# Linear attention and a leaky-ReLU MLP on one core: a new order table, other engines and ring places for its steps, and the last-but-one quarter of the result stored in two parts

## The chip, the cores and the metric

The kernel runs on one core of one Trainium2 chip. The metric is device time in microseconds of one execution. The kernel before took 276.14 us (median of three runs, 275.97 to 276.53). Comparisons below are made against that median; the trace comes from one profiled execution of its own.

## The reference

Two stages run one after the other. The first is linear ("cosformer") attention over 8 batches, 8 heads, 576 positions and 64 features:

```
r = relu(x);  phi(x) = [r*cos(theta_s), r*sin(theta_s)]        # 128 features, for q and k
kv  = einsum('bhsf,bhsd->bhfd', phi(k), v);  z = sum_s phi(k)
out = einsum('bhsf,bhfd->bhsd', phi(q), kv) / (phi(q).z + 1e-6)
```

The second takes the result as 4608 tokens of 512 features through an MLP of width 2048:

```
h = x @ w_in;  g = max(0.01*h, h);  result = g @ w_out
```

Inputs and result are float32 in DRAM; the kernel multiplies in float16 and accumulates in float32.

## The kernel before

**Tiling.** The 4608 tokens are cut into nine groups. Groups 0 to 7 are the first 512 positions of one batch each; group 8 collects the last 64 positions of all eight batches. Each group passes through the same stages, and several groups are in flight at once. Group 0 uses plain matmuls (its first MLP layer is `ffn1`, its second `ffn2`). Groups 1 to 8 use a scheme with seven block products instead of eight for each MLP layer (`ffn1s`, `ffn2s`), with sums of blocks made ahead of them and behind them on the vector engines.

**What sets the order.** The kernel is written as some 1430 named steps, and the string `ORDER` lists the names. The loop at the end of the kernel issues each step in that order, so `ORDER` fixes the order of instructions on every engine's own queue. A name can carry an engine (`:D` VectorE, `:A` ScalarE, `:P` GpSimd) and a place (`@n`) in a ring of buffers; a step that takes a place waits until the former user of that place is done. Each engine works strictly down its list: an instruction that waits holds up all behind it. SyncE (SP) issues nearly all DMAs, in the order of the table too.

**Names of the steps used below.** The first number is the group.

- `i.n`: one matmul of zeros (128x512, `ps_idle`, L298), which keeps TensorE busy while data are awaited. `idle(14)` issues fourteen of them before the table begins.
- `Lq`, `Lk`, `Lv`, `Lw1`, `Lw2`: first loads of q, k, v and the two weights; `lq`, `lk`, `lv`: those of later groups (`lq8.0` to `lq8.3`: group 8's rows of q, two DMAs each). `cw`, `w`: casts of the weights to float16; `w3.2` is the cast of the last piece of `w_out`, which `Lw2.3.2` loads.
- `rq`, `rk`, `q`, `kt`, `v`: relu, angles and casts of q, k and v. `kv`, `ko`: the sum over positions and its copy out.
- `qT`: DMA transpose of q's features. `n`, `N`: the attention's product on TensorE and its division on VectorE (`den`, `rden`, `xs`). `xT`: DMA transpose of a group's attention output into the layout that the MLP reads (group 1 does it on TensorE: `xt`, and `xo` copies it out).
- `X`: sums of blocks of xT. `fg.u.1` to `fg.u.7`: the seven products of the first layer for quarter u of the width; `b`, `s`, `u` copy accumulators, `y`, `z` add them, `a`, `c`, `e`, `d` apply the leaky ReLU and write g.
- `S`: sums of blocks of g. `T1` to `T4`: sums of blocks of w_out, made once. `Fg.n.tt.h`: half h of product n for half tt of the tokens in the second layer, four matmuls each. `M`: a sum kept for later; `O`: a quarter of the result copied or added into SBUF; `D`: its store.

**Group 8's end.** Its four result quarters are `O8.2`, `O8.5`, `O8.4`, `O8.3`. `O8.5` and `O8.3` are made and stored in two halves (`result_apart`, `store_apart`), since their accumulators lie apart; `O8.2` and `O8.4` are made whole (`result`, `store`). A store of group 8 is two DMAs, one issued by SP and one by ScalarE.

Of the kernel before, what the change touches and what calls it, by code (L numbers as in the profile page):

```python
# [31 lines left out]
Lk0.0@2 rk0.0:A Lq0.0@1 Lq0.1 Lv0.0@3 kt0.0.0 rq0.0:A qt0.1.0@1 i.6@1 kt0.0.1 rq0.1:D v0.0:D Lv0.1  # L32
Lk0.1 v0.1:P qo0.1.0:A rk0.1:A i.2@1 qt0.0.0@1 qo0.0.0:D i.8@0 i.10@0 i.4@0 i.11@0 qt0.0.1 i.14@0
qo0.0.1:A Lk0.3 rk0.3:P i.7@0 qt0.1.1@0 i.5@1 i.9@1 kt0.1.1 kt0.1.0 Lv0.2 kv0.0 i.13@0 Lk0.2 Lv0.3
v0.2:A i.12@0 ko0.0:A kt0.3.1 rk0.2:D kt0.3.0 kt0.2.1 kt0.2.0 n0.0.0@1 i.1@1 v0.3:A qo0.1.1:A kv0.1
n0.1.0@0 Lw1.3 Lw1.0@1 Lw1.1 ko0.1:A N0.0.0 N0.1.0 cw.0:P i.15@1 cw.1:P xt0.0.0@0 i.0@1 n0.1.1
# [6 lines left out]
rk1.1:D q1.0.0:D W1.1:D W1.2:D w0.0:A w0.2:P Lw2.1@2 Lv1.0 w1.2:P f0.11 w1.0:D F0.0.0@0 e0.5 e0.4
W1.3:D F0.0.2 F0.2.0 F0.3.0 F0.1.0@1 qt1.3@1 qo1.3:A qt1.2@0 F0.3.2 F0.2.2 qt1.0@1 F0.2.4 F0.0.4
F0.0.6 W0.3:D kt1.1.1 F0.2.6 qo1.2:A v1.0:A F0.3.4 kv1.0@0 kt1.1.0 W1.4:D W0.2:D qo1.0:A Lw2.2@0
F0.3.6 qt1.1@1 w2.0:A ko1.0:A Lv1.1 F0.2.8 n1.1.0@0 F0.0.8 F0.3.8 w2.2:D W0.4:D N1.1.0 F0.3.10
Lw2.3.0 Lw2.3.2 lq2@3 w3.2:D w3.0:P v1.1:A qo1.1:A kv1.1@1 F0.2.10 n1.0.0@0 ko1.1:A F0.3.12 F0.3.14
n1.0.1@1 T1 O0.3:A@0 rq2.1:P rq2.0:A q2.3.0:P F0.0.10 F0.0.12 F0.2.12 q2.2.1:P q2.0.1:P F0.2.14
# [48 lines left out]
q7.3.1:P q7.1.0:A f5.1.3 F4.2.1.1 F4.6.1.1 z5.1 M4.6 D3.3 D2.3 lv7.1 D3.4 kt7.0.0 q7.3.0:P q7.2.1:P
f5.0.4 f5.2.5 d5.0 O4.2:A@2 s5.2:A f5.1.4 n6.2 N6.2 kt7.0.1 F4.7.0.0 F4.7.0.1 F4.5.0.0@0 d5.1 c5.1
e5.1 f5.2.1 b5.2:A n6.3 f5.2.3 F4.5.0.1 f5.3.1 f5.2.6 u5.2:A f5.2.2 a5.2 N6.3 F4.7.1.0 F4.5.1.0
S4.4b F4.7.1.1 z5.2 M4.7 F4.5.1.1 f5.2.7 f5.3.5 F4.4.1.0 kt7.1.0 e5.2 b5.3:A y5.2 O4.5@3 kt7.1.1  # L100
v7.1:P lq8.1@0 f5.3.6 f5.3.2 u5.3:A s5.3:A rq8.0:A F4.4.0.0 F4.4.1.1 D4.2 q7.2.0:P q7.0.0:P c5.2
f5.3.7 F4.4.0.1 S5.1a S4.4a xT6 qT7.0 lq8.3@1 qT7.1 lq8.2@2 rq8.1:P q8.1.1:P kv7 f5.3.3 f5.2.4 a5.3
# [37 lines left out]
def kernel(  # L140
# [746 lines left out]
    def store_apart(g, n, tt):  # L887
        store_tail(2 * (n == 5) + tt, 1, st["osb", g, n, tt])
# [232 lines left out]
```

## Time and profile before

| | |
|---|---|
| median of 3 runs | 276.14 us |
| the profiled execution's own time | 276.79 us |
| its span (first to last instruction) | 275.0 us |
| TensorE matmul busy | 264.5 us, 96% |
| TensorE weight load busy | 227.5 us, 83% |
| VectorE busy | 219.6 us, 80% |
| ScalarE busy | 180.7 us, 66% |
| GpSimd busy | 90.5 us, 33% |

The span is 1.8 us shorter than the execution's own time; that part lies around the program. The shares are means over stages that differ: the loads fill the first 50 us, then VectorE and ScalarE are nearly full for some 20 us, and then TensorE runs almost without a break to the end. So the stage tables, the chain of waits and the timeline say more than the shares. In the timeline a row has the start, the length, the engine, the kernel's line, the operation, the tiles, how many instructions it merges, and in brackets the idle time before it and what ended that. "SPq" is SyncE's DMA queue.

### The profile page before, as it was taken

The page shows a single profiled execution, that of the slowest core. Times are in us where ns is not written, and L with a number is a line of the kernel's source. Part 1 is how long each engine was busy: PE and PEld are TensorE (multiplying, and loading weights), DVE is VectorE, ACT ScalarE, POOL GpSimd, SP SyncE. Part 2 cuts the span into 40 slices and gives each one's busy share as a digit, 9 for nine tenths or more (in the row PEclk, how much of TensorE's full clock was granted, in tenths as well). Part 3 has the DMA queues.
Part 4 walks back from the last instruction along what each step waited for, and adds up shares of the span by engine and source line. Part 5 has one row for each costly group of instructions (what it writes and reads, how often), then busy time and mean ns, then how long its engine had stood idle before and what let it go on. Part 6 is the DMA issues. An engine that isn't in the chain of part 4 may idle for free.

```text
span 275.0 us, 7300 instructions
## 1 busy us (share of the span) xinstructions
PE 264.5 (96%) x2991; PEld 227.5 (83%) x2991; DVE 219.6 (80%) x428; ACT 180.7 (66%) x301; POOL 90.5 (33%) x100
## 2 busy tenths in 40 slices
PE   8999899999999999999999999889999999999994
PEld 3467456579899999999999999779999999999983
DVE  4681797799998998999888988688889758768752
ACT  6465786899967788886656787547655547573400
POOL 1233231745928505903932259144000003100000
PEclk9999999999999999999999999999999999999999
DMA  6999999999999999968995893997513041400026
GB/s 206 375 391 379 400 336 347 390 200 279 288 204 314 319 246 257 320 134 186 345 232 120 270 293 114 197 183 197 117 44 74 2 91 65 153 16 25 2 76 191
DMA packets 77264, 57.61 MB, mean 209 GB/s; under 512 B 49456, under 2 KB 65840, under 8 KB 76848
## 3 DMA queue, kind: packets, MB, share of 16 engines
q1 hardware_dynamic: 76624, 56.63, 73.7%
q10 hardware_dynamic: 608, 0.52, 0.7%
q8 instruction: 23, 0.38, 0.5%
q14 instruction: 9, 0.07, 0.1%
HBM read 36.70 MB, written 9.44 MB: 168 GB/s over the span
## 4 chain that ended last, share of the span: by engine, by line
PE 74%; DVE 10%; DMA 9%; SPq 2%; ACT 2%; issue 1%; POOL 1%; DVEq 0%; ACTq 0%
PE ps L850 32%; PE ps_f L767 32%; DMA w2st<-in_moe_w_out_dram 4%; DMA ext<-in_moe_w_out_dram 4%; PE ps_idle L298 3%; DVE xs L563 2%; PE ps_num L547 2%; PE ps_kv L447 2%; DVE kp L398 1%; PE ps_f L850 1%; DMA qtl<-in_q_dram 1%; DVE ext L680 1%; DVE y L680 1%; DVE ps_f L680 1%; DVE T L680 1%
## 5 line engine op out<-in xcount | busy, mean ns | idle before, releaser
L791 ACT ACTIVATE g<-ps_f 128x512 f16<-128x512 f32 x96 | 55.7, 601 | 20.8 <-DVE ps_f L680 10.7
L850 PEld LDWEIGHTS <-g 128*128 128x128 f16 x640 | 61.9, 98 | 6.3
L850 PE MATMUL ps<-w,g 128*128 128x256 f16 x496 | 65.1, 273 | 0.0
L767 PEld LDWEIGHTS <-w 128*128 128x128 f16 x512 | 55.5, 113 | 3.9 <-issue 2.3
L767 PE MATMUL ps_f<-xT,w 128*128 128x256 f16 x384 | 55.8, 273 | 0.3 <-DVE xT L425 0.3
L767 PEld LDWEIGHTS <-wext 128*128 128x128 f16 x384 | 41.7, 113 | 1.6 <-ACT ps_f L423 0.4
L850 PE MATMUL ps<-T,ext 128*128 128x256 f16 x240 | 32.4, 273 | 0.2 <-DVE ext L680 0.2
L680 DVE TENSOR_TENSOR ps_f<-ps_f,u 128x512 f32<-128x512 f32 x32 | 22.2, 694 | 9.1 <-PE ps_f L767 6.5
L767 PE MATMUL ps_f<-X,wext 128*128 128x256 f16 x192 | 28.5, 273 | 0.3 <-ACT ps_f L423 0.3
L850 PEld LDWEIGHTS <-ext 128*128 128x128 f16 x256 | 24.7, 98 | 2.9 <-DVE ext L680 0.3
L680 DVE TENSOR_TENSOR y<-ps_f,s 128x512 f32<-128x512 f32 x32 | 22.0, 687 | 6.0 <-PE ps_f L767 2.7
L423 ACT COPY u<-ps_f 128x512 f32<-128x512 f32 x28 | 16.4, 587 | 13.5 <-PE ps_f L767 13.0
L791 ACT ACTIVATE g<-y 128x512 f16<-128x512 f32 x32 | 20.3, 633 | 7.4 <-DVE y L680 7.4
L423 ACT COPY ps_f<-ps_f 128x512 f32<-128x512 f32 x29 | 16.7, 574 | 7.1 <-PE ps_f L767 6.5
L767 PE MATMUL ps_f<-X,w 128*128 128x256 f16 x128 | 19.3, 273 | 1.5 <-DVE y L680 1.5
L563 DVE TENSOR_TENSOR xs<-ps_num,rden 128x512 f16<-128x512 f32 x28 | 19.4, 691 | 1.0
L413 POOL TENSOR_SCALAR qp<-qst,sin_t 128x512 f16<-128x512 f16 x20 | 16.0, 810 | 10.0 <-ACT qst L388 9.8
L398 DVE TENSOR_TENSOR kp<-kst,ang 128x1152 f16<-128x1152 f16 x24 | 19.3, 831 | 0.0
L767 PE MATMUL ps_f<-xT,wext 128*128 128x256 f16 x128 | 19.3, 273 | 0.0
L413 POOL TENSOR_SCALAR qp<-qst,cos_t 128x512 f16<-128x512 f16 x18 | 17.7, 987 | 3.4 <-DMA qpT<-qp 3.2
L423 ACT COPY s<-ps_f 128x512 f32<-128x512 f32 x25 | 14.7, 589 | 5.8 <-PE ps_f L767 5.8
L850 PE MATMUL ps<-ext,g 128*128 128x256 f16 x128 | 17.7, 272 | 0.0
(128 smaller groups left out, 423.6 us busy)
## 6 DMA issues: line engine op xcount, KB each, us to landing
out_dram<-osb SPq DMA_DIRECT2D x32, 256.0 KB, 3.0
qst<-in_q_dram SPq DMA_DIRECT2D x7, 1024.0 KB, 9.5
kst<-in_k_dram SPq DMA_DIRECT2D x6, 1152.0 KB, 6.8
vst<-in_v_dram SPq DMA_DIRECT2D x12, 576.0 KB, 7.9
w2st<-in_moe_w_out_dram SPq DMA_DIRECT2D x3, 1024.0 KB, 8.0
ext<-in_moe_w_in_dram SPq DMA_DIRECT2D x4, 512.0 KB, 10.2
kst<-in_k_dram SPq DMA_DIRECT2D x4, 288.0 KB, 8.0
vst<-in_v_dram SPq DMA_DIRECT2D x4, 288.0 KB, 7.8
```

The lines of the kernel that those rows point to most:

```text
L298: nc.tensor.matmul(ps, lhsT=blank[:, 0:P], rhs=blank)
L398: nc.vector.tensor_tensor(out=st["kp", b][:, lo:hi, :, f * D : (f + 1) * D].rearrange("p c j (x y) -> p (c j) x y", y=2), in0=halved("k", ...
L413: eng.tensor_scalar(out=o, in0=i, scalar1=col, scalar2=1.0, op0=ALU.mult, op1=ALU.mult)
L423: nc.scalar.copy(o, i)
L447: nc.tensor.matmul(ps[:, o, (c - lo) * NE : (c - lo + 1) * NE], lhsT=st["kp", b][sl, c, j, :], rhs=vm[sl, c, j, :], start=(j == 0), stop=( ...
L547: nc.tensor.matmul(ps[lo:hi, h // 4, (h % 4) * NE : (h % 4 + 1) * NE], lhsT=qpT[:, h, lo:hi], rhs=kv[b][:, h, :],)
L563: nc.vector.tensor_tensor(out=xs, in0=ps[:, :, 0 : 4 * NE].rearrange("p a (b e) -> p a b e", e=NE)[:, :, :, 0:D], in1=rden.rearrange("p (a ...
L680: eng.tensor_tensor(out=o, in0=a, in1=b, op=op)
L767: nc.tensor.matmul(ps[:, mi * HT : (mi + 1) * HT], lhsT=a[:, c, 2 * r0 + mi : 512 : 4], rhs=b[:, c], start=(n in (1, 5) and mi == 0 and c ...
L791: nc.scalar.activation(g_tile(g)[:, m : m + 2, r * HT : (r + 1) * HT], {"a": A, "c": y22, "e": E, "d": B_}[e].rearrange("p (m t) -> p m t" ...
L850: nc.tensor.matmul(ps[:, tt], lhsT=a[:, i, tt * P : (tt + 1) * P], rhs=b[:, i], start=(first and i == 0), stop=(i == NPR - 1 and (apart or ...
```

## The change

The string `ORDER` is replaced as a whole: nearly all steps stand at new places, many go to another engine, and many take another place of their ring. The steps themselves, the matmuls (2991) and the loads are the same but for one: `O8.4` and `D8.4` are now made and stored in two halves as well. Their buffers come from the ring of the output tiles of the earlier groups, so that `O8.4.0` takes the place that group 7's last quarter had.

Over the whole program VectorE has 442 operations instead of 428, ScalarE three fewer, GpSimd 90 instead of 100.

```
@@ ORDER (first and last lines of the table) @@
-Lk0.0@2 rk0.0:A Lq0.0@1 Lq0.1 Lv0.0@3 kt0.0.0 rq0.0:A qt0.1.0@1 i.6@1 kt0.0.1 rq0.1:D v0.0:D Lv0.1
+i.12@0 i.0@0 Lk0.0@2 Lq0.0@3 rq0.0:A qt0.1.0@1 i.11@0 qt0.0.0@0 i.10@1 rk0.0:P Lk0.2 Lq0.1 rq0.1:P
...
-F8.3.0.1 D8.3.1 O8.3.0@3 D8.3.0
+D8.3.1
@@ group 8's last quarters @@
     def result_apart(g, n, tt):
-        osb = out_tile(g, HC)
+        osb = out_tile(0 if n == 4 else g, HC)
         st["osb", g, n, tt] = osb
         part = slice(tt * HC, (tt + 1) * HC)
-        tt_op(osb, chain(g, n, tt)[0][:, tt], {5: t3, 3: t2}[n][:, part], ALU.add)
+        tt_op(osb, chain(g, n, tt)[0][:, tt], {5: t3, 3: t2, 4: t1}[n][:, part], ALU.add)
     def store_apart(g, n, tt):
-        store_tail(2 * (n == 5) + tt, 1, st["osb", g, n, tt])
+        store_tail(2 * (n != 3) + tt, int(n != 4), st["osb", g, n, tt])
...
-                    if g == NG - 1 and n in (3, 5):
+                    if g == NG - 1 and n in (3, 4, 5):
                         step(f"O{g}.{n}.{tt}", result_apart, g, n, tt)
                         step(f"D{g}.{n}.{tt}", store_apart, g, n, tt)
...
-                elif g < NG - 1 or n in (2, 4):
+                elif g < NG - 1 or n == 2:
```

Three places of the order matter below. **The first** is ScalarE's queue where the last weights arrive and group 1 begins. Before, from the copy of group 1's q to its first `s`:

```order
L423 COPY qpT<-ps_qt 128x1024
L423 CAST kv_164<-ps_kv 128x2x2x66
L423 COPY osb<-ps_o 128x512
L388 ACTIVATE qst<-qst 128x16x64
L423 COPY osb<-ps_o 128x512 x2
L411 ACTIVATE qp<-qst,cos_t 128x8x64 x2
L411 ACTIVATE qp<-qst,sin_t 128x8x64
L423 COPY xT<-ps_xth 128x2x256
L388 ACTIVATE kst<-kst 128x18x64
L411 ACTIVATE qp<-qst,sin_t 128x8x64
L423 COPY s_178<-ps_f_934 128x512
```

The same stretch of the changed kernel (`w_106<-ext` are the casts `w3.0` and `w3.2`, `osb` group 0's results):

```order
L423 COPY qpT<-ps_qt 128x1024
L423 CAST w_106<-ext 128x1024 x2
L423 CAST kv_164<-ps_kv 128x2x2x66
L423 COPY osb<-ps_o 128x512 x2
L388 ACTIVATE qst<-qst 128x16x64
L411 ACTIVATE qp<-qst,sin_t 128x8x64
L411 ACTIVATE qp<-qst,cos_t 128x8x64 x3
L388 ACTIVATE kst<-kst 128x18x64
L411 ACTIVATE qp<-qst,sin_t 128x8x64
L423 COPY s_178<-ps_f_931 128x512
```

The two casts of the last weights came to ScalarE (from GpSimd and VectorE); group 0's two result copies that free TensorE's accumulators now stand directly behind each other, ahead of q's relu, and one `osb` and the copy of `xT` left for VectorE.

**The second** is SP's queue ahead of group 6's transpose `xT6` (`xT<-xs`; `qtl` are the loads `lq8`, `qpT` the transposes `qT`, `out_dram` result stores). Before, from `lv7.1` on:

```order
L247 DMA vst<-in_v_dram 128x2x576
L908 DMA out_dram<-osb 128x2x256
L254 DMA qtl<-in_q_dram 64x8x64 x2
L908 DMA out_dram<-osb 128x2x256
L503 DMA_TRANSPOSE xT<-xs 128x16x128
L491 DMA_TRANSPOSE qpT<-qp 128x16x128
L254 DMA qtl<-in_q_dram 64x8x64 x2
```

The same stretch of the changed kernel, from `lv7.1` on:

```order
L247 DMA vst<-in_v_dram 128x2x576
L908 DMA out_dram<-osb 128x2x256
L491 DMA_TRANSPOSE qpT<-qp 128x16x128
L254 DMA qtl<-in_q_dram 64x8x64 x4
L908 DMA out_dram<-osb 128x2x256 x2
L503 DMA_TRANSPOSE xT<-xs 128x16x128
```

`qT7.0`, a second pair of `qtl` loads and a second store now stand ahead of `xT6`. In the changed kernel the first `qtl` load takes the place of group 7's k, which is free after `kt7.1.0`, the step that follows `N6.3` on VectorE; before, it took that of group 7's v, free after the cast `v7.1` on GpSimd.

**The third** is the end of VectorE's queue. Before (`ps_f` are the accumulators of `O8.5` and `O8.3`, `ps` with a number that of `M8.7` and `O8.4`):

```order
L680 TENSOR_TENSOR ext<-ps_4217,ext 128x512 x2
L680 TENSOR_TENSOR osb<-ps_f_934,ext 128x256
L680 TENSOR_TENSOR g<-g,ext 128x4x256 x2
L680 TENSOR_TENSOR osb<-ps_4217,ext 128x512
L680 TENSOR_TENSOR osb<-ps_f_933,ext 128x256
L680 TENSOR_TENSOR osb<-ps_f_934,ext 128x256
L680 TENSOR_TENSOR osb<-ps_f_933,ext 128x256
```

The same end of the changed kernel:

```order
L680 TENSOR_TENSOR ext<-ps_4224,ext 128x512
L680 TENSOR_TENSOR osb<-ps_f_930,ext 128x256
L680 TENSOR_TENSOR g<-g,ext 128x4x256
L680 TENSOR_TENSOR osb<-ps_4224,ext 128x256
L680 TENSOR_TENSOR osb<-ps_f_931,ext 128x256
L680 TENSOR_TENSOR osb<-ps_f_930,ext 128x256
L680 TENSOR_TENSOR osb<-ps_4224,ext 128x256
L680 TENSOR_TENSOR osb<-ps_f_931,ext 128x256
```

The 128x512 result became two of 128x256, and the two halves of `O8.3` now have the second half of `O8.4` between them.

More of the change, by code (lines that the diff above doesn't have):

```diff
@@ L31 @@
 ORDER = """
-Lk0.0@2 rk0.0:A Lq0.0@1 Lq0.1 Lv0.0@3 kt0.0.0 rq0.0:A qt0.1.0@1 i.6@1 kt0.0.1 rq0.1:D v0.0:D Lv0.1
[L33 to L36, printed above, removed]
@@ L43 @@
[L43 to L48, printed above, removed]
@@ L97 @@
[L97 to L102, printed above, removed]
@@ new lines @@
+Lk0.3 qt0.1.1@0 i.1@1 i.9@0 Lw1.1 Lv0.2 rk0.2:P kt0.2.0 Lv0.3 kt0.2.1 kt0.1.1 rk0.3:D v0.0:A v0.1:P
+Lw1.2 Lw1.3 kt0.3.0 kt0.3.1 i.14@1 qo0.0.1:A i.4@0 i.15@0 kv0.0 i.13@1 qo0.1.1:A ko0.0:A n0.0.0@1
+i.7@1 v0.3:A n0.1.0@0 N0.0.0 Lw1.5 Lw1.7 Lw1.4 v0.2:P kv0.1 i.6@0 cw.3:P N0.1.0 ko0.1:A cw.0:A i.5@0
+n0.0.1@1 N0.0.1 xt0.1.0@0 xt0.0.0@1 n0.1.1 cw.1:A xo0.0.0:A xt0.0.1@1 xo0.1.0:D cw.2:A f0.0.a@1
+f0.1.a f0.1.b f0.2.a@0 N0.1.1 f0.2.c xo0.0.1:D cw.7:P cw.4:P f0.1.c i.2@0 f0.3.a f0.3.d f0.2.d
+xt0.1.1@1 f0.0.c f0.3.c f0.1.d xo0.1.1:D f0.3.e f0.0.b f0.0.d f0.2.e f0.0.e f0.4.a f0.1.e e0.1 e0.0
@@ new lines @@
+F0.0.6 F0.3.6 F0.3.8 F0.2.8 ko1.0:A w2.2:A qo1.1:A F0.2.10 n1.1.0@1 F0.3.10 F0.0.8 N1.1.0 Lw2.3.0
+w3.0:A F0.2.12 F0.3.12 Lv1.1 n1.0.0@0 N1.0.0 v1.1:P kv1.1@1 Lw2.3.2 W1.4:P w3.2:A T1 lq2@0 F0.3.14
+F0.2.14 ko1.1:A O0.3:A@1 O0.2:A@2 rq2.1:A rq2.0:P q2.0.1:A n1.0.1@1 q2.3.0:P F0.0.10 F0.0.12 N1.0.1
+F0.0.14 F0.1.2 n1.1.1 O0.0:D@3 N1.1.1 F0.1.4 xt1.0.1@1 xo1.0.1:D xt1.0.0@0 xt1.1.0@1 xo1.0.0:D
+xo1.1.0:D xt1.1.1@1 xo1.1.1:D X1.1:D X1.3:D q2.2.0:A q2.1.0:A q2.0.0:A F0.1.6 lk2@1 q2.2.1:P rk2.1:P
+f1.0.1 X1.2:P b1.0:D rk2.0:A kt2.0.0 f1.0.5 q2.1.1:A f1.1.1 F0.1.8 s1.0:A q2.3.1:A f1.0.6 lk3@3
@@ new lines @@
+u5.0:A X5.4:D v7.0:A f5.0.3 z5.0 S4.1c S4.2a F3.3.0.1 F3.3.1.1 f5.0.2 F4.1.0.0@0 f5.1.1 S4.3c S4.3b
+e5.0 a5.0 b5.1:A n6.0 f5.0.7 F4.1.0.1 f5.1.5 F4.1.1.0 y5.0 F4.1.1.1 f5.1.2 f5.0.4 rq7.0:A s5.1:A
+q7.0.1:P d5.0 q7.0.0:D O3.3@0 rk7.1:P rk7.0:P q7.1.0:P S4.2c f5.1.6 N6.0 u5.1:D F4.6.0.0@1 F4.6.1.0
+M4.1:A q7.3.1:P f5.1.3 z5.1 f5.2.1 v7.1:P q7.1.1:A c5.0 e5.1 b5.2:A q7.3.0:A n6.1 f5.1.7 F4.6.1.1
+F4.2.0.0 F4.2.1.0 f5.2.6 N6.1 f5.2.2 F4.2.1.1 F4.6.0.1 n6.2 kt7.0.0 kt7.0.1 y5.1 N6.2 M4.6 F4.2.0.1
@@ new lines @@
+u5.2:A a5.1 f5.2.5 kt7.1.1 S4.4a f5.2.7 O4.2:A@1 F4.5.0.0@0 F4.5.1.0 F4.5.1.1 s5.2:A f5.2.3 F4.7.1.0
+n6.3 F4.5.0.1 F4.7.0.0 f5.1.4 a5.2 c5.1 y5.2 z5.2 N6.3 e5.2 d5.1 f5.3.5 F4.7.0.1 F4.7.1.1 f5.3.1
+kt7.1.0 qT7.0 lq8.0@0 lq8.1@2 D3.5 f5.2.4 D3.3 xT6 M4.7 kv7 O4.5@3 S4.4b S5.1a c5.2 s5.3:A b5.3:A
+f5.3.3 F4.3.1.0 f5.3.6 F4.4.0.0 F4.3.0.0 S5.1b F4.3.0.1 ko7:A rq8.1:A u5.3:A d5.2 f5.3.7 F4.4.1.0
+F4.4.0.1 f5.3.2 z5.3 S5.2a X6.1:D X6.3:D y5.3 f6.0.1 F4.4.1.1 f5.3.4 e5.3 a5.3 f6.0.5 n7.0 F4.3.1.1
+X6.2:P d5.3 s6.0:A q7.2.0:P q7.2.1:P q8.1.1:P b6.0:D f6.0.6 O4.4@0 D4.5 qT7.1 lq8.3@3 rq8.0:A u6.0:A
@@ L136 @@
+F8.3.0.0 F8.3.0.1 O8.3.0@0 D8.3.0 F8.4.1.0 F8.4.1.1 O8.4.1@2 D8.4.1 F8.3.1.0 F8.3.1.1 O8.3.1@3
+D8.3.1
 """
```

164 lines of the change are left out of this document (78 added, 86 removed).

## The prediction

> **What bounds the kernel now.** The page's shares say TensorE, 96%, but a share is a mean, so I read first the view that gives the busy time of each engine by stretch. I cut it at 35 us (group 0's second layer begins), 53.3 (group 1's first product), 75.9, 168 and 187. A row has the stretch, its length, and busy us of PE, PEld, DVE, ACT and POOL, then the granted clock, DMA share and GB/s.
>
> ```profile
> 0.00:35.00 35.00, 31.14 (x295) 17.31 (x296) 20.24 (x53) 21.52 (x29) 9.73 (x20) 1.00 0.97 350
> 35.00:53.30 18.30, 17.78 (x209) 10.21 (x208) 15.66 (x31) 13.99 (x19) 6.55 (x7) 1.00 1.00 354
> 53.30:75.90 22.60, 22.25 (x330) 19.46 (x330) 21.55 (x39) 21.72 (x38) 15.26 (x15) 1.00 1.10 266
> 75.90:168.00 92.10, 92.10 (x1113) 87.08 (x1114) 83.24 (x162) 68.47 (x119) 44.11 (x45) 1.00 0.96 250
> 168.00:187.00 19.00, 16.99 (x224) 15.43 (x223) 14.65 (x27) 10.67 (x20) 7.82 (x10) 1.00 0.78 157
> 187.00:271.00 84.00, 84.00 (x828) 77.99 (x825) 63.80 (x119) 44.31 (x81) 7.02 (x7) 1.00 0.29 75
> ```
>
> The reader is to see where TensorE is *not* busy: 3.86 us before 35, 0.52 up to 53.3, 0.35 up to 75.9, none for 92 us, 2.01 between 168 and 187, none again for 84 us. No order can make the two stretches without a gap shorter, since the matmuls are the same; it can only add gaps there. What an order can win lies before 75.9, where DMA (97% and more) and then DVE and ACT (21.55 and 21.72 of 22.60) are full, and in the 2.01 us.
>
> Second, the chain of waits, for what sets the start of the full part (start, length, what):
>
> ```profile
> 36.36 9.76 DMA ext<-in_moe_w_out_dram
> 46.13 0.70 DVE w L425
> 46.96 1.23 DVE T L680
> ```
>
> The last weights land at 46.12 (36.36 + 9.76); the cast `w3.2` and the sum `T1` follow at once. The change loads the same bytes ahead of them, and its last weight load hangs on the same steps, so I keep 46.1 as a fixed point. What happens before it counts only if TensorE then lacks work.
>
> **Part 1: the start, up to 46 us.** The zero matmuls fill TensorE's waits:
>
> ```profile
> 1.19 5.49 PE L298 MATMUL ps_idle<-blank 128*128 128x512 f16 x14 [1.19 <-DVE blank L293]
> 8.92 1.69 PE L298 MATMUL ps_idle<-blank 128*128 128x512 f16 x4
> ...
> 25.07 4.91 PE L627 MATMUL ps_h<-xT,w 128*128 128x512 f16 x22
> ```
>
> A product of the same size takes 4.91/22 = 0.22 us; the four zero matmuls take 1.69/4 = 0.42 each, since each waits for the one before it. There are 30 before and after. The change puts two ahead of the first product (it starts some 0.8 us later) and five in a row ahead of `kv0.0` (2.1 us). By my count group 0 then starts up to 1.5 us later, but its last four blocks of the first layer wait for `e0.6` behind q's relu, which wait for a load in both. TensorE has filler from group 0's second layer, so I take 0. Between 0 and the 1.5 us of later start; if the filler is gone it appears as waiting at 46 us.
>
> The granted clock is 1.00 in all rows. The Trainium skill (TensorE: Matmul & The Clock Gate, "HAM oscillation — how this bites in real kernels") says that a gap of over some 3.4 us halves the clock again. By it the sum would be the same here, unless the change's wait for the second half of q, about 1.9 us by my count, grew; no row of this trace shows such a gap.
>
> **Part 2: the last weights to group 1, 46 to 76 us.** Rows of before, timeline:
>
> ```profile
> 46.13 0.69 DVE L425 CAST w<-ext 128x1024 f16<-128x1024 f32 x1 [0.99 <-DMA ext<-in_moe_w_out_dram]
> ...
> 50.15 1.06 ACT L423 COPY osb<-ps_o 128x512 f32<-128x512 f32 x2
> ...
> 50.77 0.42 PE L582 MATMUL ps_numh<-kv,qpT 128*128 128x66 f16 x8 [0.32 <-ACT osb L423]
> ...
> 51.22 0.17 DVE L558 TENSOR_SCALAR den<-ps_numh 128x8 f32<-128x8 f32 x1 [0.96 <-PE ps_numh L582]
> ...
> 57.01 0.70 DVE L680 TENSOR_TENSOR ps_f<-ps_f,u 128x512 f32<-128x512 f32 x1 [0.31 <-PE ps_f L767]
> ```
>
> Before, the last division of group 1 (`N1.1.1`, 51.22) waits for its product (50.77), and that for ACT's copy of group 0's result (the second of the two at 50.15), which stood behind q's relu. After, `w3.2` is on ACT, which casts a 128x1024 piece in 1.05 (the row of such a cast at 16.14):
>
> ```profile
> 16.14 1.05 ACT L423 CAST w<-wext 128x1024 f16<-128x1024 f32 x1
> ```
>
> So it ends at 46.12 + 1.05 = 47.17, 0.35 later than before. From 47.2 TensorE runs `F0.3.14`, `F0.2.14`, `n1.0.1` and four more steps of `F0`, each two matmuls of 0.22: 6 x 0.43 + 0.25 = 2.85, so `n1.1.1` at 50.05. The copies are done by then (48.9). DVE: `T1` 47.2 to 48.4, `N1.0.1` to 49.6, the copy `O0.0` behind `F0.0.14` to 50.5, `N1.1.1` at 50.55 against 51.22: **0.67 earlier**. From there DVE has the same sums, and DVE and ACT are full (95 and 96%), so I let the lead reach 75.9 and take **-0.7**. What is queued behind the late cast on ACT is `ko1.1`, which `n1.0.1` needs; TensorE comes to that only at 48.1, so it is not late. The ends: -1.1 (one more DVE gap of 0.31, the row at 57.01, closes too) and 0 (ACT puts the cast `v2.1` ahead of `u1.1`, on which DVE's `z1.1` waits; at 1.17 for such a cast, less the filler `T3` that moved ahead, the lead is gone).
>
> **Part 3: group 6's transpose, 168 to 187 us.** Rows of before: DVE's division `N6.3` and sum `kt7.1.0`, SP, then DVE and PE.
>
> ```profile
> 168.13 0.69 DVE L563 TENSOR_TENSOR xs<-ps_num,rden 128x512 f16<-128x512 f32 x1
> ...
> 178.20 0.43 DVE L680 TENSOR_TENSOR X<-xT 128x512 f16<-128x512 f16 x1 [2.18 <-DMA xT<-xs]
> ```
>
> ```profile
> 170.55 1.31 SPq L254 DMA_DIRECT2D qtl<-in_q_dram  x2
> 171.97 0.57 SPq L908 DMA_DIRECT2D out_dram<-osb  x1
> 172.64 3.40 SPq L503 DMA_TRANSPOSE xT<-xs  x1
> ```
>
> ```profile
> 179.28 0.60 PE L767 MATMUL ps_f<-X,w 128*128 128x256 f16 x4 [1.52 <-DVE y L680]
> ...
> 186.32 0.60 PE L767 MATMUL ps_f<-xT,w 128*128 128x256 f16 x4
> ...
> 187.63 0.60 PE L767 MATMUL ps_f<-xT,w 128*128 128x256 f16 x4
> ```
>
> `N6.3` is done at 168.82, but SP is held by the `qtl` load and issues `xT6` at 172.64. It lands and frees `X6.1` at 178.20, 5.56 us after issue; `y5.3` stands behind `X6.1`, and `f5.3.4` waits 1.52 for it. That is most of the 2.01.
>
> After: the queue ahead of `xT6` has two pairs of `qtl` (1.31 each) and two stores (0.57 each), with the gaps between them 3.9. They start when `kt7.1.0` ends, which is 1.13 + 0.7 = 1.8 after `N6.3` starts on DVE; `xT6` is issued 5.7 after that start and lands at 5.7 + 5.56 = 11.3. TensorE has, from `n6.3` to `f6.0.1` (now the first to need it), 18 steps of 0.437 (1.31/3, from 186.32 to the third step after it at 187.63), `kv7` (1.1) and `n6.3` (0.25): 9.2, which is 8.7 after `N6.3` starts. So `f6.0.1` waits some 2.6. The quickest such transpose with loads around it is group 5's:
>
> ```profile
> 144.87 1.79 SPq L503 DMA_TRANSPOSE xT<-xs  x1
> ...
> 149.22 1.17 POOL L680 TENSOR_TENSOR X1b<-xT 128x512 f16<-128x512 f16 x1 [9.13 <-DMA xT<-xs]
> ```
>
> Its 4.35 gives a landing at 10.05 and a wait of 1.35. `y5.3`, behind two sums of 0.43, adds 0 to 0.6. Against 2.01 the change is between -0.7 and +1.2; by the nearest row, the same transpose's own 5.56, +0.6 at least. I take **+0.3**, between that and the quick one, since SP then has no late GpSimd cast ahead.
>
> **Part 4: the full stretches.** Before, DVE has 83.24 of 92.10 us (90%) without a gap on PE. The change gives DVE 14 more operations: six copies at 0.7, the rest small, some 7 us in all, so the share rises to some 93%, against 95% in the stretch 53.3 to 75.9, where PE lost 0.35. By the order DVE's list grows most between the first products of groups 5 and 6 (43 steps instead of 36) and of groups 3 and 4 (40 instead of 38). So between 0 and 2 x 0.35 = 0.7; I take **+0.1**, nearer the row of 92 us with none.
>
> **Part 5: the end.**
>
> ```profile
> 269.32 1.91 PE L850 MATMUL ps_f<-w,g 128*128 128x256 f16 x16
> ...
> 271.32 0.42 DVE L680 TENSOR_TENSOR osb<-ps_f,ext 128x256 f32<-128x256 f32 x1 [0.50 <-PE ps_f L850]
> ```
>
> The last sum follows the last matmul (269.32 + 1.91 = 271.23) by 0.09, and its store follows it. After, the last piece has the same size, and the store before it is 0.87 earlier (two steps), longer than a store's 0.57 on SP. The split removes one 128x512 sum from a place where PE did not wait. **0**; if the extra store held up SP, at most its 0.57.
>
> **The sum:** -0.7 + 0.3 + 0.1 = -0.3. The profiled execution took 276.79 (span 275.0 and 1.8 around it), 0.65 over the median; I lay the difference on the median: 276.14 - 0.3 = **275.8 us**.
>
> **The rivals.**
> - *Both early parts pay in full.* `xT6` is as quick as group 5's, DVE's small gap closes, no new wait comes: -1.1 - 0.7 + 0 gives 274.3. For it: SP is held by a VectorE step and not by a late GpSimd cast. Against: two pairs of loads stand ahead. 0.26.
> - *`xT6` comes later than before* (slower). The transpose's row on SP (3.40, against 1.79 for group 5's) says that it may wait for the transfers ahead; with one more store there (0.57) it lands at 11.9, `f6.0.1` waits 3.2 and `y5.3` 0.6: +1.8, with the lead and the small waits 276.14 + 1.8 - 0.7 + 0.1 = 277.3. It decides from a landing at 11.3 with `y5.3`'s 0.6 in full (+1.2 - 0.7 + 0.1 = +0.6). 0.24.
> - *The lead is lost on ACT* (`v2.1` ahead of `u1.1`): 0 + 0.3 + 0.1 gives 276.5; the new order then does nothing at the start. 0.10.
> - *The clock falls in the start.* The first 14 zero matmuls take 5.49/14 = 0.39 each, the products at 25 us 0.22; if such a slow spell of 5 us came back after the longer wait for q, TensorE would lose 2.2, less some 1.0 by which my count has it ready ahead of the last cast: 275.8 + 1.2 = 277.0. For it: only that wait. Against: 1.00 in all rows. 0.03. The Trainium skill's page on the clock gate, named in part 1, has the rule.
>
> **How the numbers follow.** My sum has 0.37 (own range 275.3 to 276.4). 0.2% is 0.55 us, about what a measurement of this kernel can tell from no change: faster is under 275.6, slower over 276.7. Faster: 0.26 and 0.14 of the sum's 0.37, 0.40. Same: the other 0.23 and the lost lead's 0.10, 0.33. Slower: 0.24 and 0.03, 0.27. The range reaches to 274.2 and 277.5, both big rivals with little beyond.
>
> **What would show it.** Right: `N1.1.1`'s division starts near 50.5 and the first `F1.6` product near 75.1 (75.84 before); `f6.0.1` shows an idle time of 1 to 3 us; no other idle over 0.5 us after 76; the last sum follows the last matmul by 0.1. Wrong: the cast of the last weights starts later than 46.3, or TensorE waits there; `f6.0.1` has no idle time; DVE waits for ACT's `u` before 65 us; or TensorE's idle time between 76 and 168 exceeds 0.5.

## The result, and the profile after

The changed kernel takes **279.49 us** (median of 7 runs, 276.82 to 283.31) against 276.14: ratio 1.0108, 95% interval 1.0059 to 1.0156. The ratio compares means and leaves out the one slow run of 283.31, whose mean granted clock was 0.986. The changed kernel is slower, and outside the forecast's range (274.2 to 277.5). Its profiled execution took 279.06 us, with a span of 277.2.

The same view as in the forecast, busy time by stretch, of the changed kernel, at the same cuts (start:end, length, busy us of PE, PEld, DVE, ACT, POOL, then granted clock, DMA share, GB/s):

```profile
0.00:35.00 35.00, 32.84 (x309) 18.88 (x310) 20.73 (x52) 23.91 (x31) 14.11 (x24) 1.00 0.98 353
35.00:53.30 18.30, 17.22 (x206) 10.57 (x204) 16.86 (x31) 13.54 (x19) 11.61 (x10) 1.00 1.03 367
53.30:75.90 22.60, 22.51 (x333) 19.56 (x331) 22.09 (x40) 20.74 (x36) 8.97 (x10) 1.00 1.15 245
75.90:168.00 92.10, 90.51 (x1093) 85.56 (x1092) 81.33 (x166) 70.48 (x120) 36.82 (x37) 1.00 0.98 251
168.00:187.00 19.00, 15.65 (x212) 14.12 (x210) 13.11 (x26) 9.41 (x18) 4.15 (x5) 1.00 0.43 102
187.00:271.00 84.00, 84.00 (x834) 78.11 (x833) 66.87 (x129) 42.88 (x78) 5.20 (x6) 1.00 0.37 85
```

The reader is to see three things. The start has less idle time on TensorE (35.00 - 32.84 = 2.16 us, before 3.86). The 92 us in which TensorE never waited now have a gap of 92.10 - 90.51 = 1.59. And the stretch with group 6's transpose has 3.35 instead of 2.01. Behind 271 there are 6.2 us of span instead of 4.0.

The first gap in the timeline of TensorE (start, length, engine, what, in brackets the idle time ahead and what ended it), and SP's rows around it, after and then before the change. `qpT` rows are the transposes qT2.0 and qT2.1, the `vst` row lv3.0 and lv3.1, the `qst` row behind it lq4, the `xT` row xT2, and the `out_dram` row ahead of xT2 the store D0.2:

```profile
79.85 1.03 PE L767 MATMUL ps_f<-xT,w 128*128 128x256 f16 x8 [1.59 <-DMA xT<-xs]
```

```profile
57.99 5.82 SPq L491 DMA_TRANSPOSE qpT<-qp  x1
63.86 0.57 SPq L665 DMA_DIRECT2D out_dram<-osb  x1
64.61 1.94 SPq L247 DMA_DIRECT2D vst<-in_v_dram  x2
66.59 0.47 SPq L237 DMA_DIRECT2D qst<-in_q_dram  x1
71.63 4.72 SPq L503 DMA_TRANSPOSE xT<-xs  x1
```

```profile
58.81 5.82 SPq L491 DMA_TRANSPOSE qpT<-qp  x1
64.74 1.03 SPq L247 DMA_DIRECT2D vst<-in_v_dram  x2
65.94 0.37 SPq L237 DMA_DIRECT2D qst<-in_q_dram  x1
66.36 1.20 SPq L665 DMA_DIRECT2D out_dram<-osb  x1
72.07 3.12 SPq L503 DMA_TRANSPOSE xT<-xs  x1
```

TensorE's `f2.0.1` before the change, with no idle time ahead of it:

```profile
78.91 1.04 PE L767 MATMUL ps_f<-xT,w 128*128 128x256 f16 x8
```

xT2 is issued 0.44 earlier than before (71.63, 72.07), yet TensorE's first product of group 2, `f2.0.1`, waits for it until 79.85. By the trace's record of when transfers complete it landed at 79.8, before the change at 77.3. Before, that was 1.6 ahead of `f2.0.1` (78.91): a reserve that no row of idle time shows. After, it lands 2.5 later and TensorE would be there 0.65 earlier (79.85 - 1.59 = 78.26), which uses the 1.6 up and leaves the wait of 1.59. What moved in SP's rows is D0.2, from behind lq4 to ahead of the v loads.

The second place, TensorE's three waits near 180, and ACT and SP there (`qtl` rows are lq8.0 and lq8.1, the first row of ACT is `rq8.1`, the second `u5.3`):

```profile
179.43 0.60 PE L767 MATMUL ps_f<-xT,w 128*128 128x256 f16 x4 [2.04 <-ACT u L423]
...
182.19 0.63 PE L767 MATMUL ps_f<-xT,w 128*128 128x256 f16 x4 [0.86 <-DMA xT<-xs]
...
183.71 0.60 PE L767 MATMUL ps_f<-X,w 128*128 128x256 f16 x4 [0.45 <-DVE y L680]
```

```profile
178.27 0.63 ACT L388 ACTIVATE qtl<-qtl 128x512 f16<-128x512 f32 x1 [2.99 <-DMA qtl<-in_q_dram]
178.81 0.57 ACT L423 COPY u<-ps_f 128x512 f32<-128x512 f32 x1
```

```profile
172.45 3.42 SPq L254 DMA_DIRECT2D qtl<-in_q_dram  x4
175.92 1.14 SPq L908 DMA_DIRECT2D out_dram<-osb  x2
177.10 3.35 SPq L503 DMA_TRANSPOSE xT<-xs  x1
```

The waits are at `f5.3.7`, `f6.0.1` and `f5.3.4`: 2.04 + 0.86 + 0.45 = 3.35. The first is for ACT, which had put the relu of a load that came late ahead of `u5.3`; the second is for xT6, issued 177.10, 4.65 behind the first of the `qtl` loads.

The third place, the end (DVE's last sums, and the stores on SP and ACT's queue):

```profile
270.68 0.96 DVE L680 TENSOR_TENSOR osb<-ps_f,ext 128x256 f32<-128x256 f32 x2
270.80 3.73 SPq L899 DMA_DIRECT2D out_dram<-osb  x6
270.80 4.04 ACTq L899 DMA_DIRECT2D out_dram<-osb  x6
...
272.96 0.42 DVE L680 TENSOR_TENSOR osb<-ps_f,ext 128x256 f32<-128x256 f32 x1 [0.45 <-PE ps_f L850]
```

All six pairs of stores go out in one row from 270.80, at 0.62 each on SP. The last sum is done at 272.96 + 0.42 = 273.38, its stores are issued at 273.98 on SP and 274.29 on ACT's queue. Before the change the last store followed its sum by 0.04.

### The profile page after: what moved, and what is told of

Its sections match the earlier page's. It is cut to its first block, busy times and chain, and to the rows that moved or that the text cites. A ratio compares the mean times of both kernels' runs of the same rounds, so it can differ in the third digit from the quotient of the medians.

```text
span 277.2 us, 7299 instructions
## 1 busy us (share of the span) xinstructions
PE 264.6 (95%) x2991; PEld 228.3 (82%) x2991; DVE 222.4 (80%) x442; ACT 181.0 (65%) x298; POOL 80.9 (29%) x90
## 4 chain that ended last, share of the span: by engine, by line
PE 74%; DMA 8%; DVE 8%; ACT 4%; SPq 2%; issue 1%; POOL 1%; DVEq 0%
PE ps_f L767 32%; PE ps L850 29%; DMA xT<-xs 5%; DMA ext<-in_moe_w_out_dram 4%; PE ps_idle L298 4%; PE ps_num L547 2%; PE ps_h L627 2%; PE ps_kv L447 2%; DVE xs L563 1%; DVE kp L398 1%; PE ps_f L850 1%; SPq L254 1%; ACT g L791 1%; POOL qp L413 1%; PE ps_qt L523 1%
## 5 line engine op out<-in xcount | busy, mean ns | idle before, releaser
L767 PE MATMUL ps_f<-xT,w 128*128 128x256 f16 x384 | 54.9, 273 | 4.6 <-DMA xT<-xs 2.5
L423 ACT COPY ps_f<-ps_f 128x512 f32<-128x512 f32 x27 | 15.4, 570 | 6.7 <-PE ps_f L767 6.1
L680 DVE TENSOR_TENSOR osb<-ps,ext 128x512 f32<-128x512 f32 (+1 forms) x24 | 15.9, 664 | 2.6 <-PE ps L850 2.4
L423 ACT COPY s<-ps_f 128x512 f32<-128x512 f32 x24 | 14.1, 585 | 4.3 <-PE ps_f L767 3.2
L423 ACT COPY u<-ps_f 128x512 f32<-128x512 f32 x25 | 14.7, 587 | 3.3 <-PE ps_f L767 3.1
L650 PE MATMUL ps_o<-w,g 128*128 128x512 f16 x64 | 15.6, 379 | 0.4 <-ACT w L423 0.4
```

Source lines behind the costliest of these rows:

```text
L423: nc.scalar.copy(o, i)
L650: nc.tensor.matmul(st["ps_o", g, tt], lhsT=st["g", g][:, m, tt * P : (tt + 1) * P], rhs=w2[:, m, :], start=(m == 0), stop=(m == NFT - 1),)
L680: eng.tensor_tensor(out=o, in0=a, in1=b, op=op)
L767: nc.tensor.matmul(ps[:, mi * HT : (mi + 1) * HT], lhsT=a[:, c, 2 * r0 + mi : 512 : 4], rhs=b[:, c], start=(n in (1, 5) and mi == 0 and c ...
```

## The experiments

Theory A: the time went at these three places, each by where a DMA stands in a queue: xT2 behind D0.2 and the loads, xT6 behind the loads and stores, the last stores behind D8.4.0. The rivals: chance of one execution (B in the first run), a wait that only moves elsewhere (B), ACT's relu as the cause near 180 (C). "Lost time" in the expectations is the distance between two starts on TensorE less the first one's own time (0.109 us for a product of 256 columns).

**The changed kernel again, unaltered.**

> The changed kernel again, unaltered, as the base of the next runs and to see which of its waits repeat. Theory A (the waits come from the order): f2.0.1 waits 1.3 to 2.0 us near 79.9 again, the region of f5.3.7, f6.0.1 and f5.3.4 loses 3.3 to 3.9, the last store goes 0.6 to 0.9 after the last sum; time 278.5 to 280. Rival B (the waits are chance of the DMA transfers in one execution): f2.0.1 waits under 0.7, or the waits stand elsewhere, at the same time.

279.23 us (278.92 to 280.13; ratio to the kernel before 1.0116, 1.0073 to 1.0158). In its profile:

```profile
81.42 1.03 PE L767 MATMUL ps_f<-xT,w 128*128 128x256 f16 x8 [1.52 <-DMA xT<-xs]
180.88 0.60 PE L767 MATMUL ps_f<-xT,w 128*128 128x256 f16 x4 [1.92 <-ACT u L423]
183.31 0.63 PE L767 MATMUL ps_f<-xT,w 128*128 128x256 f16 x4 [0.53 <-DMA xT<-xs]
184.83 0.60 PE L767 MATMUL ps_f<-X,w 128*128 128x256 f16 x4 [0.45 <-DVE y L680]
```

The same waits stand at the same steps: they come from the order, not from chance. The wait at `f2.0.1` is 1.45 to 1.64 in all five profiles of orders that put D0.2, the v loads and lq4 ahead of xT2 in this order. xT2 landed 16.2 after the end of qT2.1 on SP, 16.0 in the first profile.

**xT6 ahead of the loads and stores.**

```
- z5.2 N6.3 ... kt7.1.0 qT7.0 lq8.0@0 lq8.1@2 D3.5 f5.2.4 D3.3 xT6 M4.7 ... ko7:A rq8.1:A u5.3:A
+ z5.2 qT7.0 N6.3 xT6 ... kt7.1.0 lq8.0@0 lq8.1@2 D3.5 f5.2.4 D3.3 M4.7 ... ko7:A u5.3:A ... s6.0:A rq8.1:A
```

> Group 6's block transpose xT6 is issued right behind N6.3 instead of behind two pairs of qtl loads and two stores, and rq8.1, ACT's relu of one of these loads, behind s6.0 instead of ahead of u5.3. Theory A: xT6 is issued near 172 and lands near 176.5, before TensorE reaches f6.0.1 (near 179); the waits at f5.3.7 (2.04), f6.0.1 (0.86) and f5.3.4 (0.45) go, TensorE's lost time between 170 and 190 falls from 3.9 to about 0.6, and the time is 2.5 to 3.3 lower than the changed kernel's, 276.0 to 277.0. Rival B: the loads moved behind the transpose are now late (rq8.1, qT7.1 and group 7's later halves, or xT7), and 1 us or more of it is given back before 205; time 277.5 or more.

276.28 us (274.30 to 277.58; ratio 0.9992, 0.9955 to 1.0029), 3.0 below the changed kernel run again. `qT7.0` is moved up with it, so that it still goes out ahead of xT6. SP and TensorE in its profile:

```profile
172.55 1.91 SPq L503 DMA_TRANSPOSE xT<-xs  x1
174.56 3.29 SPq L254 DMA_DIRECT2D qtl<-in_q_dram  x4
```

```profile
179.20 1.04 PE L767 MATMUL ps_f<-xT,w 128*128 128x256 f16 x8
...
180.51 0.60 PE L767 MATMUL ps_f<-X,w 128*128 128x256 f16 x4
```

None of the three waits is left; lost time between 170 and 190 is 0.51, against 3.78 in the changed kernel run again (some 4.2 in its first profile). As expected by A; nothing was given back later. xT6 was expected to land near 176.5 and landed at 178.8, only 0.4 ahead of `f6.0.1` (179.20): there is little reserve left.

**Only the relu `rq8.1` later.**

```
- ko7:A rq8.1:A u5.3:A
+ ko7:A u5.3:A ... s6.0:A rq8.1:A
```

> Only rq8.1, ACT's relu of the late qtl load, goes behind s6.0; xT6 stays behind both load pairs and the two stores. Theory A (the landing of xT6 sets the loss): f5.3.7 no longer waits, but f6.0.1 then waits 2.5 to 3.2 for xT6 instead of 0.7 to 0.9, TensorE's lost time between 170 and 190 stays within 0.5 of the changed kernel's 3.5 to 3.9, time within 0.5 of 279.3. Rival C (the relu in front of u5.3 is the cause): the 2.1 to 2.2 at f5.3.7 go and nothing takes their place, time 277 to 277.5.

280.54 us (279.57 to 281.33; ratio 1.0151, 1.0116 to 1.0185). TensorE, and then the busy view of the stretch behind the wait:

```profile
183.15 0.63 PE L767 MATMUL ps_f<-xT,w 128*128 128x256 f16 x4 [2.47 <-DMA xT<-xs]
```

```profile
180.00:183.00 3.00, 0.68 (x7) 0.41 (x4) 0.00 (x0) 0.60 (x1) 0.00 (x0) 1.00 0.99 184
183.00:184.00 1.00, 0.85 (x8) 0.78 (x9) 0.84 (x3) 0.00 (x0) 0.21 (x1) 0.95 0.61 215
184.00:187.00 3.00, 2.72 (x20) 1.91 (x19) 1.81 (x4) 1.03 (x2) 2.36 (x3) 0.50 0.02 5
```

The wait at `f5.3.7` is gone and stands at `f6.0.1` instead, 2.47 for xT6. So xT6 sets the loss and C falls. The time was expected within 0.5 of 279.3 and is 1.2 higher; the kernel before, measured beside it, took 276.49 here and 276.01 beside the runs above, so some 0.8 is this kernel's own. Behind the one long wait the granted clock is 0.50 for 3 us: lost time between 170 and 190 is 4.89, 1.1 more than in the changed kernel run again, where at most 0.5 was expected. All four runs of this kernel had a mean clock of 0.993 or 0.994.

**Only the store D0.2 behind lq4.**

```
- qT2.0 lq3@0 ... qT2.1 D0.2 T2 ... lv3.0@2 lv3.1 ... lq4@1 y1.2 ... O0.1:A@2 ... O1.2@0
+ qT2.0 lq3@0 ... qT2.1 T2 ... lv3.0@2 lv3.1 ... lq4@1 D0.2 y1.2 ... O0.1:A@0 ... O1.2@2
```

> Only the store D0.2 (256 KB) is moved from ahead of the loads lv3.0, lv3.1, lq4 to behind them, as it stands before the change (result tiles in ring places 0 and 2 exchanged from O0.1 on, so that O0.1 doesn't wait for the store). The same bytes then go ahead of xT2, in the old order. Theory A1 (the store behind the transpose qT2.1 holds the loads up): lq4 lands 2 us earlier, counted from the end of qT2.1 on SP (13 before the order is put back, 9.6 in the kernel before the change), xT2 lands 12.6 to 13.5 after it instead of 16, and f2.0.1 waits under 0.3: time 1.3 to 1.8 lower, 277.5 to 278.0. Rival A2 (the bytes count, not their order): xT2 lands 16 after the end of qT2.1 again, no change.

279.95 us (279.31 to 280.76; ratio 1.0132, 1.0100 to 1.0165). SP, TensorE and DVE:

```profile
66.90 0.58 SPq L665 DMA_DIRECT2D out_dram<-osb  x1
71.71 3.90 SPq L503 DMA_TRANSPOSE xT<-xs  x1
```

```profile
76.72 2.78 PE L850 MATMUL ps<-T,ext 128*128 128x256 f16 x24 [1.13 <-DVE osb L680]
79.34 1.04 PE L767 MATMUL ps_f<-xT,w 128*128 128x256 f16 x8
```

```profile
75.97 0.69 DVE L680 TENSOR_TENSOR osb<-ps,ext 128x512 f32<-128x512 f32 x1 [1.56 <-DMA out_dram<-osb]
```

xT2 did what A1 says: it landed at 77.6, 13.2 after the end of qT2.1, and `f2.0.1` no longer waits; lq4 came 1.3 earlier (11.4 after that end instead of 12.7), not the expected 2. The time did not follow. The edit made a wait of its own: the sum `O1.2` now takes the ring place that D0.2 frees, waits 1.56 for that store, and TensorE waits 1.13 for the sum. And near 180 the three waits are 2.08 + 1.59 + 0.45 = 4.12 in this profile, against 3.35 and 2.90 in the two of the changed kernel; whether the exchanged ring places cause that is not shown. So the order of the same bytes sets when xT2 lands (A2 falls), but the expected 277.5 to 278.0 was missed. That the order is worth time shows in the joint edits below, most clearly in the last, which moves the store without the new wait; no run has that alone.

**lq4 behind the transposes.**

```
- n2.1 lq4@1 y1.2 ... rq4.0:A rq4.1:A q4.0.0:P ... qT3.1 ... rk4.0:P rk4.1:P f2.0.1 b2.0:A
+ n2.1 y1.2 ... qT3.1 lq4@1 ... rk4.0:P rk4.1:P rq4.0:A rq4.1:A q4.0.0:P ... f2.0.1 b2.0:A
```

> The 1 MB load lq4 is issued behind qT3.1 instead of ahead of group 2's block transpose xT2, with its relus on ACT and POOL's six steps on it behind rk4.1. Theory A: xT2 no longer waits for lq4 (landed 76.5); it waits for the v loads alone (72.2), ends on SP near 73.5 and lands near 76, so the 1.75 at f2.0.1 is gone and the time is 1.3 to 1.8 lower than the changed kernel's: 277.5 to 278. Rival B: xT2 takes as long on SP (4 us or more) without the load, since its own 512 KB set that, and f2.0.1 waits 1 us or more: time unchanged within 0.5. Rival C: the late lq4 makes qT4.0, group 4's first products or xT3 late and the gain is given back before 130.

292.00 us (290.56 to 292.71; ratio 1.0566, 1.0514 to 1.0618). SP, then TensorE and ACT:

```profile
72.02 1.88 SPq L503 DMA_TRANSPOSE xT<-xs  x1
```

```profile
78.32 1.04 PE L767 MATMUL ps_f<-xT,w 128*128 128x256 f16 x8
...
90.93 1.01 PE L767 MATMUL ps_f<-X,wext 128*128 128x256 f16 x4 [11.14 <-ACT ps_f L423]
```

```profile
88.39 2.00 ACT L388 ACTIVATE qst<-qst 128x1024 f16<-128x1024 f32 x2 [13.15 <-DMA qst<-in_q_dram]
```

The half of A that speaks of xT2 holds: without lq4 ahead it holds SP 1.88 instead of 4.72, and `f2.0.1` does not wait. But the relus of lq4 stood ahead of group 2's first copy on ACT, and everything there waited 13.15 for the load; TensorE waited 11.14, and the granted clock was 0.50 from 82.0 to 95.7. That is worth seeing for itself: an engine that works strictly down its list pays for a load that nobody on the critical path needs.

**The stores at the end early.**

```
- O8.5.0@1 S8.4b F8.5.1.1 F8.4.0.0 F8.4.0.1 O8.4.0@3 O8.5.1@2 D8.4.0 D8.5.1 D8.5.0
+ O8.5.0@1 D8.5.0 S8.4b F8.5.1.1 O8.5.1@2 D8.5.1 F8.4.0.0 F8.4.0.1 O8.4.0@3 D8.4.0
```

> At the end, the stores D8.5.0 and D8.5.1 go out behind their own sums, ahead of D8.4.0, and the sum O8.5.1 is moved ahead of O8.4.0 on DVE. Theory A: the six pairs of stores no longer stand in one row from 270.8; the last store follows the last sum by 0.1 instead of 0.6 to 0.9, and the stretch from the last matmul's start to the end falls from 4.57 to about 4.0: 0.5 to 0.9 lower than the changed kernel's. Rival B: each store's own transfer sets the end and the row of stores is hidden: no change (within 0.2).

277.88 us (276.44 to 280.26; ratio 1.0058, 1.0024 to 1.0093). From the last matmul's start to the end of the span it takes 3.90 instead of 4.57: 0.67, within what A expects (B falls). The medians differ by 1.35, but the runs of both kernels spread over more than that, so the 0.67 of the profile is the figure to keep.

**The old order with the split alone.** The kernel before the change, `O8.4@2` replaced by `O8.4.0@1 O8.4.1@2` and `D8.4` by `D8.4.0 D8.4.1`.

> The kernel before the change with its last quarter O8.4 and D8.4 in two parts and nothing else. Theory A (the store queue, not the split itself, cost 0.5 in the changed kernel): here one more pair of stores stands ahead of D8.5.0, D8.3.1 and D8.3.0; the last store goes out 0.1 to 0.6 later than its sum: the stretch from the last matmul's start to the end 4.05 to 4.6, time 276.0 to 276.7. Rival: the split is free (4.05), because the earlier part's store is out before.

276.42 us (274.61 to 277.59; ratio 0.9983, 0.9955 to 1.0012); 4.18 from the last matmul's start to the end, against 4.05. The split itself costs 0.13 of the 0.52; the rest came from where the stores were put.

**The old order with xT6 ahead.** The kernel before the change, `xT6` moved from behind `lq8.1@0` and `D4.2` to right behind `N6.3`.

> The kernel before the change with one edit: xT6 is issued behind N6.3, ahead of lq8.1 and D4.2. Theory A (the forecast's reading of the 2.01 us between 168 and 187): xT6 is issued near 169.5 and lands near 174, X6.1 no longer holds y5.3, the 1.68 at f5.3.4 goes, and with it 1.5 to 2.5 us: 273.6 to 274.6. Rival: something else holds f5.3.4 or n7.0 (ACT's d5.2, DVE's sums), and less than 0.5 is won.

274.46 us (274.03 to 275.55; ratio 0.9916, 0.9881 to 0.9950); the kernel before, measured beside it, took 276.62. SP, then TensorE:

```profile
168.32 1.92 SPq L503 DMA_TRANSPOSE xT<-xs  x1
```

```profile
178.55 0.43 PE L547 MATMUL ps_num<-kv,qpT 128*128 128x66 f16 x8 [0.56 <-DMA qpT<-qp]
```

The wait at `f5.3.4` is gone; 0.56 at `n7.0` is new, for qT7.0, which now stands behind. This is the forecast's reading of the 2.01 us, shown.

**Three edits together.** First xT6 ahead, stores early and D0.2 behind lq4; then the same with lq4 behind qT3.1 in place of D0.2's move, and its relus on ACT later still; then with D0.2 between lv3.1 and lq4.

> The edits of the runs before together: xT6 ahead with rq8.1 late, the stores at the end early, D0.2 behind lq4. Theory A: the gains add up, 279.3 - 3.0 - 0.7 - 1.6 = 274.0, 0.992 of the kernel before the change. If A2 holds for the store: 275.6. Rival B: one of the waits comes back elsewhere, 275.5 or more although f2.0.1 doesn't wait.

274.33 us (273.47 to 275.06; ratio 0.9925, 0.9898 to 0.9953). The gains add up, but for 0.79 at `F1.5.0.0`, again for `O1.2`.

> xT6 ahead with rq8.1 late, the stores at the end early, and lq4 behind qT3.1 with its two relus on ACT behind d2.1 and a2.2, so that group 2's steps on ACT no longer stand behind the load. Theory A: f2.0.1 and f2.0.6 don't wait, 279.3 - 3.0 - 0.7 - 1.6 = 274.0. Rival C: POOL's six steps on the late lq4 end near 100 instead of 87; if qT4.0 or X3.2 becomes late by it, group 3 or 4 waits 0.5 to 2 us between 100 and 130 and the time is 274.5 to 276.

275.63 us (274.57 to 276.82; ratio 0.9977, 0.9956 to 0.9998). `f2.0.1` does not wait. Instead TensorE waits 0.84 near 95.7 for ACT, which now does the relus in the middle of group 2, and 0.51 at `kv4` near 99.0 for DVE, whose k product waits for POOL's relu of the load lk4, now behind lq4. C was right in kind, not in place.

> As the run with three edits and the store, but D0.2 goes between lv3.1 and lq4, so that it lands earlier and the sum O1.2, which takes its place in the ring, needn't wait (F1.5.0.0 waited 0.95 to 1.3 behind that sum). Theory A: D0.2 lands near 73, xT2 as before near 78.4, neither F1.5.0.0 nor f2.0.1 waits over 0.3: 273.2 to 273.6. Rival: with the store ahead of lq4 again, lq4 and with it xT2 come 1 us later and f2.0.1 waits instead; 274.3 unchanged.

**273.60 us** (272.27 to 275.12; ratio 0.9889, 0.9853 to 0.9925): faster than both kernels. The store goes out early enough that `O1.2` does not wait for its place, and `f2.0.1` does not wait for xT2. The busy view of its fourth and fifth stretch:

```profile
75.90:168.00 92.10, 92.10 (x1115) 87.20 (x1113) 83.38 (x169) 70.60 (x121) 36.76 (x37) 1.00 1.02 248
168.00:187.00 19.00, 19.00 (x248) 17.81 (x245) 15.78 (x34) 12.52 (x23) 5.72 (x8) 1.00 0.77 175
```

TensorE waits in neither. Its new order beats the old one with xT6 ahead by its median only (0.9889 and 0.9916, the intervals overlap).

## Why the prediction was wrong

The sum was -0.7 + 0.3 + 0.1 + 0 and should have been about -0.4 + 1.3 + 1.6 + 0.5 = +3.0. The ratio of 1.0108 is 3.0 us; from the start of the last weights' cast to the end of the span the two profiles differ by 232.0 - 228.9 = 3.1. The largest miss is part 4, where a new wait of 1.59 stood against a term of 0.1.

- **Part 1, the start: right in what counts.** Group 0 starts 0.9 later (18.67 against 17.77). The wait of its last blocks (1.07 ahead of `f0.8` before) vanished (the load `Lq1` lands 1.7 earlier), and the idle time up to 35 us fell by 1.70. As forecast, that is worth nothing, since group 1 waits for the last weights. That "fixed point" of 46.1 is not fixed: the cast `w3.2` could start at 45.2 here, at 43.65 to 46.13 in three profiles of the old order and at 44.76 to 47.08 in ten of the new. This alone moves single executions by some us; whether the new order makes it later on average is open, but the 3.1 above lie behind it.
- **Part 2, the lead: right, a little small.** From the start of `w3.2`'s cast to `N1.1.1`'s division it takes 49.85 - 45.21 = 4.64, before 51.22 - 46.13 = 5.09: 0.45 for the forecast 0.67. In all profiles it is 4.39 to 4.66 in the new order (ten) and 5.09 to 5.84 in the old (three), so the lead belongs to the order. At group 1's first second-layer product, `F1.6`, 0.33 of it is left. It was then lost at `f2.0.1`, as any lead would have been. Which of the moved steps made the lead was not tried apart.
- **Part 3, xT6: the mechanism right, the size wrong.** Forecast: issued 5.7 after `N6.3` starts on DVE (170.64), landing at 11.3, wait of 2.6 and up to 0.6 for `y5.3`. Measured: 6.5, 11.5, 2.04 + 0.86 = 2.90 and 0.45. That the landing came out so close is partly luck, since two errors cancel: the queue ahead took 4.65 instead of 3.9 (the four loads 3.42 instead of 2.62), and xT6 landed 5.05 after its issue instead of 5.56. The step of this part that failed is the last one, "I take +0.3, between that and the quick one, since SP then has no late GpSimd cast ahead": the nearest row gave +0.6 at least, the time was +1.3. The quick row (4.35 from issue to landing) was given a weight, and the longer queue ahead was not. The relu `rq8.1` ahead of `u5.3` was overlooked, but only shows where TensorE waits, not how long.
- **Part 4, the full stretches: the step that failed.** "So between 0 and 2 x 0.35 = 0.7; I take +0.1" priced DVE's longer list alone. DVE held TensorE up nowhere there, and its share did not rise to 93%: it was busy 81.33 of 92.10 us, 88%, and so less than the 90% before. The store D0.2 was moved past three loads on SP, and that was the new wait: 1.59. The row "92 us with none" was read as room, but it only says that nobody waited; xT2 had 1.6 us in hand, and the forecast never worked that out. Its own sign of being wrong, idle time over 0.5 between 76 and 168, came.
- **Part 5, the end: wrong.** "The store before it is 0.87 earlier, longer than a store's 0.57 on SP" counted one store. D8.4.0 waits for its sum (270.34 + 0.42 = 270.76), and D8.5.0, whose sum was done at 269.37, stands behind it, as does D8.5.1, whose sum stands behind D8.4.0's on DVE; so six pairs go out in a row. The bound named there, a store's 0.57, is close to what it cost, 0.52, but it was meant for one store in the way and not for a row of six: luck.
- **The rivals.** "xT6 comes later than before" was the right one for part 3 (forecast +1.8, there +1.3), but no case held the other two places. "The clock falls in the start" did come true in one profile of the changed kernel (the wait for the second half of q, 1.52 ahead of `qt0.0.1`), not in the first; there it hides behind the weights. It costs time near 180 in the profile with `rq8.1` late, where no case had put it. The Trainium skill (TensorE: Matmul & The Clock Gate, "HAM oscillation — how this bites in real kernels") names gaps of over some 3.4 us for this. The runs differ: near 180 waits of 2.20 and 2.47 were enough in two profiles and 2.04 was not in another, and at the start 1.52 was enough once.

## What to carry to other kernels

A stretch without waiting says that nothing was late, not by how much: before an order is changed, work out for each transfer how far ahead of its first use it lands, and re-price it with what is now queued in front of it. A DMA that is moved is moved past everything on its queue. A block transpose held its queue here for as long as transfers ahead of it were under way (4.72 with lq4 ahead, 1.88 without), so it should be issued the moment its data are there, with loads and stores that nobody waits for behind it. An engine that works strictly down its list must not meet the consumer of a late load ahead of work that is ready.

## What the runs showed of the hardware that was not expected

- **The granted clock halves after short waits, in some executions.** Behind a wait of 2.47 (ended 183.15) the rows above show 0.50 for 184 to 187. The profile with the stores early has it behind a wait of 2.20, the changed kernel run again behind one of 1.52 at the start:

```profile
181.21 0.60 PE L767 MATMUL ps_f<-xT,w 128*128 128x256 f16 x4 [2.20 <-ACT u L423]
```

```profile
182.00:185.00 3.00, 2.93 (x16) 1.81 (x14) 1.43 (x4) 1.12 (x2) 0.32 (x1) 0.51 0.76 170
```

```profile
10.00:11.00 1.00, 0.70 (x17) 0.54 (x17) 0.41 (x1) 1.00 (x2) 0.87 (x2) 0.86 1.02 354
11.00:14.00 3.00, 3.00 (x23) 1.48 (x22) 2.97 (x7) 2.85 (x4) 0.66 (x1) 0.50 1.04 403
```

  In the first profile of the changed kernel a wait of 2.04 had no such effect, nor had 1.92 in the second, 2.08 with the store behind lq4 and 2.09 with lq4 late. The clock records of the traces tell more: in all thirteen profiles the granted clock changes only after a whole multiple of 3.41 us (6.83, 3.41 and 262.83 in the changed kernel run again; 177.49, 3.41 and 92.16 with `rq8.1` late), and the first change lies anywhere between 3.9 and 7.2 us. Near 180 the clock fell where a wait of 2.20 or 2.47 lay whole in one such stretch. The wait of 1.92 lay whole in one too and did nothing; an edge cut those of 2.04, 2.08 and 2.09. This is read from a few profiles and was not tried by itself, and the 1.52 at the start does not fit it. The last kernel above, with no waits near 180, had mean clocks of 0.997 to 1.000 in its six runs; the changed kernel's eleven had 0.986 to 1.000.
- **The block transposes xT2 and xT6 hold SP for 1.9 us (1.88 to 1.92 in six profiles) where what was issued ahead on SP has landed by then (to 0.1 us), and for 3.1 to 5.3 where loads or stores are still under way.** In one case between, where the last load landed 0.65 behind the issue, it was 2.13. Where the trace tells the landings, the long holds end within 0.9 us of the last of them: xT2 in the changed kernel at 76.35, lq4 at 76.52.
- **One 256 KB store right behind a transpose delays the loads behind it by more than its bytes.** With the same bytes ahead, xT2 landed 15.9 to 16.2 after the end of qT2.1 with the store first (five profiles), 13.5 with the store between the v loads and lq4, and 12.6 to 13.5 with it last (five). The bytes alone would take some 0.7 us at the 353 GB/s of the first 35 us (an estimate). The DMA engines moved only 10 GB/s between 65 and 66 us in the changed kernel, but 5 with the store behind lq4 as well, so that hole is not the difference; from 67 to 70 us they moved 183, 329 and 164 GB/s, with the store behind lq4 366, 380 and 394. Why is open; no run takes it apart further.
